# An order written out by hand: 1,087 operations of a convolution and gMLP block put in another sequence

## The chip, the cores and the metric

The kernel runs on one core of one Trainium2 chip. The time is the device time of that core in microseconds (us), from the start of the launch to its end; the figure quoted is the median of three executions. A profile was taken of one further execution, and all rows and lines of a trace come from that one.

The engines of the core are called by the letters that the kernel itself uses: P is TensorE (matrix products and transposes), D is VectorE, A is ScalarE, G is GpSimd (POOL in the profile), and S is SyncE, which here only issues transfers. Each engine takes its instructions strictly in the order in which it was given them, and waits at an instruction whose operands are not ready, with everything behind it.

## What is computed

The sequence has S = 2048 tokens and D = 640 channels, the batch is one, the gMLP's inner half is Fh = 864, and everything outside is bf16. Cut to what matters:

```python
mod = (silu(c) @ w_mod).reshape(6, D)            # sa, ca, ga, sb, cb, gb
h = layernorm(x) * (1 + ca) + sa                 # x is A_q
k4 = sum(shift(k, t) * shift_k[:, 3 - t] for t in range(4))
kv = k4 * v
y = irfft(rfft(kv, 2 * S) * rfft(ssm_k, 2 * S))[:S] + kv * ssm_D
x = x + ga * h * y
h = layernorm(x) * (1 + cb) + sb
z = gelu(h @ w_in)                               # 2048 x 1728
g = w_sp @ layernorm(z[:, 864:]) + b_sp[:, None]  # the token mix
out = x + gb * ((z[:, :864] * g) @ w_out)
```

## The kernel before

**How the work is cut.** The long convolution is a Fourier transform written as matrix products. The 640 channels are five units of 128 channels (units 0 to 4). A unit's k passes four taps (a product with four diagonal matrices), is multiplied by v, regrouped by a transposing transfer, and then goes through a first transform stage, eight steps of the second stage with the product by the filter's transform, the inverse stage, and a last stage that is multiplied straight into the gate h·ga. The filter ssm_k takes the same two first stages, with ssm_D added to its first element, which stands for the term kv·ssm_D. The tables of sines and cosines are worked out on the chip at the start.

The gMLP works on four groups of four token tiles of 128. A group's layer norm, its transpose hT, the modulation by 1 + cb and sb, the product with w_in (in blocks of 128 tokens by 432 features), GELU, the statistics of the second half and its normalization follow one another. The token mix w_sp·z is done as products over 2x2 blocks, seven for every pair of output tiles in place of eight; for it sums and differences of the blocks of w_sp and of z are made first. The first pair's seven products belong to the list described next; the other seven pairs and most of the product with w_out follow it in an ordinary loop.

**What sets the order.** The program first only records 1,087 operations: each with a number (its place in the recording), the engines that may run it, what it reads and writes, and the tiles that it allocates. The list ORDER at the top of the file then gives the sequence: the letter says which engine runs the operation, the number which operation it is. `Plan.run` walks through the list, asserts that all that an operation depends on was put out before it, and issues it:

```python
for e, i in order:
    o = self.ops[i]
    assert e in o["eng"] and done.issuperset(o["deps"]), (e, i)
    o["fn"](engines[e])
```

So the list holds no times and no priorities. It decides for each engine in which order its operations come, for operations that may run on several engines which of them does it, and, since a tile of a tag with n buffers is handed out again after n allocations, which earlier readers a new tile waits for. The number of buffers of every tag is in `SLOTS`; the ones named below are `pu` and `pz` (two PSUM tiles each), `sm` (two), `s1` (one), `T` (two) and `KH` (seven).

**The operations that are named later**, by number:

- Start. P1034 and other numbers from 1033 to 1038 are filling matmuls. S2, S3, A1 and G5/D6 fetch D, c and the shift taps (A1 is a transfer that ScalarE issues) and widen D; P7, P8 and P9 turn them, A10, A11 (D_col) and A12 copy them out; A4 is one Silu activation on a scratch value (line 786). D13 to D22 make the tables of the first stage, D27 is the padding of unit 0's k and A28 its diagonal matrices of taps. Loads of k and v S23 to S26, S39, S40, S52, S64, S65 and S77; taps and v (P29 to D36 for unit 0); regrouping transfers kx (S37, S38, S51, S63, S76, S88). S89, S90, S93, S95, S97 and S99 load ssm_k, D91, D92, D94, D96, D98 and D100 add D_col to it.
- Tables of the second stage, numbers 101 to 127, in four chunks: turns (D104, D110, D116, D122), subtraction (the number after), two sines each on ScalarE, a sign (G108, G114, G120, G126) and a negation (G109, G115, G121, G127; line 357). P134, P137, P140 and P143 with A135 and their like copy and negate them into the inverse's tables. A133 is one GELU activation on a scratch value (line 815); it loads ScalarE's function table for GELU ahead of its first use.
- Convolution. P146 to A157: first stage of the filter of unit 0, with copies out of PSUM; P158 to A173: its second stage, with copies into `KH` tiles; P174 to D184: first stage of kv of unit 0. From P186 on come the steps: forward product (P186), product with the filter on VectorE (D187, line 470), where wanted two sums (csum, G188 and G189; lines 479 and 480), the inverse product (P190) and the copy zc (A191; line 504). Units 1 to 4 hold the numbers 228 to 523 in the same way; D515 is the last filter product.
- S524 to S527 load x in quarters (640 KB each, S527 the last), D528 to 549 are the first layer norm's statistics (ln1), 550 to 565 its normalization (xn). S566, S571, S576, S581, S584 and S587 load w_mod in sixths, and 567 to 591 make the six modulations of it; ghm, 592 to 599 and later, puts h, 1 + ca, sa and ga together for each unit; res adds the finished unit to x, ln2 takes the statistics of the sum.
- Transition. P716 to D723 flip the last unit's result and copy it out, P724 to P750 are its last stage, D728 to D731 and D737 multiply it into the gate, D732 to D742 add it and take statistics.
- z. For group 0: 759 to 777 statistics and normalization, P765, P766, P778 and P779 transposes, D767 to A771 and D780 to A784 the modulation of the two halves, then a product on TensorE followed by its GELU on ScalarE, in pairs (P785 and A786, P788 and A789, P792 and A793, P813 and A814, P815 and A816, P817 and A818, ...; lines 944 and 946). Groups 1, 2 and 3 turn hT by a transfer (S845, S911, S977) and modulate it with 846 to 850, 912 to 916 and 978 to 982, on three engines. G829, G895, G961 and G1027 are the rstd of the second half (line 955, two instructions on GpSimd: lines 189 and 190), D1028 the number that goes with G1027, and 1029 to 1032 group 3's normalization zn (line 967).
- Mix. S1039 to S1044 load transposed tiles of w_sp, S1045 the bias, S1046 w_out; D1055 to D1062 and D1063 to D1070 are sums of blocks of w_sp and of z (line 1021; D1063 and D1064 T1, D1065 and D1066 T2, D1067 and D1068 T3, D1069 and D1070 T4); P1071, P1073, P1075, P1077, P1078, P1082 and P1084 the first pair's seven products (line 1036), each with eight matmuls.

Of the kernel before, what the change touches and what calls it, by code (L numbers as in the profile page):

```python
# [37 lines left out]


ORDER = """  # L40
D0 P1034 A1 P7 D18 D128 D13 D15 A4 S89 D14 A16 D101 S2 G5 D6 P8 G102 D103 D116 D117 A10 A11 P1038 A28 A129 S90 D91 D17
P1035 A118 A119 S23 P146 P149 D104 S25 D105 A106 A107 D27 P1036 A147 P29 A148 P31 G108 S24 A150 G109 S26 D92 P155 D110
D111 A112 D151 A113 A156 G120 G121 P152 A154 A153 G114 D30 D32 G115 D20 P33 D122 D123 A124 A157 A125 G126 S524 D34 P35
D36 S525 D528 D529 D530 P1033 P158 A159 P162 A163 P134 P164 A135 A165 P166 A167 P137 D19 A21 P140 D141 P168 G127 S93
A169 P170 S37 S38 A171 D138 P172 A173 D94 P228 A229 D22 P174 A176 G139 P177 A179 D531 D175 D178 P234 S39 D235 G136 G41
P180 A181 D182 D532 P183 P230 A184 G53 A185 P186 D187 G142 A231 P202 D203 G42 P43 A533 D130 P232 G188 D189 S40 D44 P45
D46 S52 P196 D197 A534 G198 G199 S527 P160 A161 P190 A191 A233 P49 D50 P47 G54 D48 P212 P204 P248 S3 A535 P200 A205 P9
A249 P143 D213 G214 G215 D543 A12 G67 G131 G132 P222 A144 G145 D223 P55 D56 P192 D193 D536 G537 P59 D60 A544 A545 S51
P57 P252 A253 D58 P206 D207 G208 G209 P194 A201 S566 P218 D219 D538 G550 G551 P254 A195 A255 S526 D539 D540 P567 A568
S95 P569 A570 P258 A259 P216 P236 A237 P242 A243 G224 G225 P256 D257 P238 A217 A239 A541 P61 D62 S571 D96 S65 P210 S64  # L50
G66 P240 A241 P260 P220 D261 A211 G554 A546 P302 A303 P292 G555 G556 G557 A221 P574 G262 G263 D542 G552 D293 D547 P246
A247 P226 A227 S63 P572 P286 D287 D288 D553 P304 A305 D573 P264 A265 P250 A251 G78 P294 A295 P308 A309 D575 D652 G548
D549 G562 D592 P296 D297 G289 P276 A558 G298 P68 P306 S576 D277 P72 D615 P244 P290 A133 D559 A307 P270 D271 P326 A245
D69 P278 A291 G563 G564 P316 D73 A327 A565 D598 A317 P266 P328 A329 A279 D267 G299 P300 D301 P577 P314 S97 A315 P330
A331 G272 G273 D594 P324 A325 G613 D650 D578 S77 D593 D614 P70 D71 A560 A561 G617 P310 A311 P332 A333 G595 D714 D671
P280 D281 P74 D98 P579 D596 D75 P322 A323 P274 P350 A79 D351 G282 P376 A377 G283 P344 D345 D580 G654 A275 P268 A269
P334 D335 P378 G599 A379 P80 D597 P312 S600 A313 D81 P284 G346 G347 P320 P601 D602 A285 A321 P380 G336 G337 D708 G709
P366 A381 P370 D367 D371 P82 P382 A383 P318 G619 A319 P603 P338 P348 A349 A339 D83 S76 P388 A389 P400 D604 P605 D606
A401 S99 D100 P360 D361 P352 A353 P386 A387 P402 D620 G618 G372 G373 A403 P607 D608 P374 D375 P398 A399 G362 P354 G363
D355 G610 D356 G357 D616 P404 G653 A405 P364 P86 P384 A365 G656 P406 A407 D87 A385 P340 D341 P84 P368 D85 P408 P414  # L60
D409 A369 P450 P342 A451 P390 S621 P622 D415 G710 A391 G711 G677 D623 G410 G411 P454 A455 P418 P396 D419 A343 P624
P358 S581 P452 A397 D625 A453 G651 G420 D421 P392 P440 A393 P626 D627 P412 D441 G657 P456 A359 P428 G678 A413 G655
A457 D429 G430 G431 P628 D629 G630 P416 A417 P394 A395 P422 D423 S88 P474 A475 P464 A465 D635 P444 D445 G446 P582 A583
P480 A481 D636 P424 D425 P442 A443 D675 G676 D637 P458 A459 G447 P476 A477 D638 P434 D435 P426 D427 P472 A473 S658
P659 D660 P478 A479 P432 P466 P661 A433 P482 P448 A467 D609 D632 A449 D662 P663 G436 G437 P438 A439 P462 A463 D483
P498 D664 P665 D499 G673 G484 G485 P518 P486 D519 P502 D503 D504 P500 A501 G674 P460 A461 P468 A469 D666 P488 D489
A487 S584 G672 P585 A586 P508 G520 G521 P522 G505 A523 G668 D509 P492 D493 P506 A507 P470 A471 S679 P680 D681 P514
D515 G510 P490 A491 G511 G494 G495 P512 G715 G667 D634 A513 P682 D683 P516 A517 D631 P684 D685 P496 S757 D639 D633
P686 D687 D688 D690 A497 P720 A721 P716 G693 P722 P718 D717 P724 D719 P726 A723 P727 D689 P725 D728 G698 D729 D730
D759 D731 D760 G761 D696 D732 D733 D692 D762 G763 D735 A764 S587 P588 A589 P736 P1037 P590 A591 D734 D691 D772 D773  # L70
G774 P750 P765 D737 D738 D767 D769 D768 P766 A771 A770 D775 P743 D741 D837 G712 D697 P792 D751 S758 A777 P815 A816
D694 G776 P779 A783 A784 D742 P785 D739 D835 A786 D695 D740 P778 D836 D838 D752 A793 D713 D744 D745 G703 G839 D840
G841 G842 D843 P788 D782 A789 D781 D780 G612 D794 P795 A796 P817 P819 D670 D797 D669 D702 D700 D706 D611 G640 D642
A844 S845 D749 A818 P799 A800 G847 D641 D644 A820 D747 D902 P821 G846 D705 D701 D801 D645 D699 A822 P823 A824 D643
D904 P802 A803 D804 P806 A807 P825 A826 D805 A848 P813 A850 P827 A828 P809 A810 D849 A814 P851 A852 D746 P875 A876
D901 P879 A880 P858 A859 D748 D903 D790 D787 D811 P872 A873 D808 G905 D906 P865 S1046 P889 A866 A890 D648 P881 D704
A882 D756 D646 D812 D753 D967 D907 D909 G908 D754 D1050 P861 A862 D1047 P854 A855 D867 P893 A894 S1042 P883 A884 D798
G910 S911 P887 A888 A916 P891 A892 D877 P868 A869 D647 D968 P885 A886 D755 D969 D649 D707 D970 D1051 G971 D972 S1040
D791 S1039 A973 D976 D914 D975 D974 D853 D1052 G912 S1045 G913 G915 D856 P959 A960 P917 A918 D857 G829 D830 S977 G982
D874 D878 P947 A948 D834 D831 D860 D832 D833 D1063 D870 P920 A921 P924 A925 P938 A939 S1044 D863 D864 P931 S1041 D1055  # L80
D1056 P941 A942 D1058 D926 D979 G980 P927 A928 A932 G978 D1048 P953 D919 D933 D871 D929 P934 D940 P949 A954 D922 A981
P1000 D1054 P997 D923 S1043 A935 D936 G895 D896 D899 D1059 A950 P983 D930 A998 D999 D1060 A1001 D1002 A984 D943 D944
A898 A900 P993 A994 P1007 A1008 D937 D1057 G961 D897 D1064 D962 P1004 D985 D963 P990 P986 A987 D988 D989 A991 D992
D995 D996 A1005 D1006 P951 D1003 A952 A964 D965 P1025 P1015 A1016 D1009 D1010 A1026 D966 D1067 G1027 D1028 P955 A956
P945 A946 P957 D1030 P1021 A1029 P1013 D1032 A1022 A1014 P1071 P1073 A958 D1031 D1068 P1082 D1065 D1066 P1078 D1069
D1070 A1072 P1075 D1079 A1074 D1083 P1077 D1076 D1080 P1084 P1011 A1012 D1085 P1017 A1018 P1019 A1020 S1081 D1062
S1086 D1049 P1023 A1024 D1053 D1061
"""


# [1143 lines left out]
```

## The time and the profile before

| what | value |
|---|---|
| median of three executions | 312.26 us (312.03 to 312.69) |
| the profiled execution | 312.08 us |
| span of its instructions | 310.0 us |
| P186, the first forward product of unit 0, starts | 23.68 us |
| D515, the last filter product, starts | 119.08 us |
| D767, the first modulation of z, starts | 131.52 us |
| P1071, the first tile product, starts | 188.71 us |
| the last operation of the list on TensorE ends | 205.05 us |

The span runs from the first instruction to the last; the device time has 2.08 us more, around it. The busy time of an engine is a sum over the whole span, while the limits change by stage: what counts for a change in one stage is which engine is full there and which wait ends last there. The profile page cuts the span into 40 slices with the busy tenths of each engine. The view by windows gives the busy time of each engine in stretches that one chooses. Overlapping matmuls are pipelined, so that TensorE's work is best taken from the spacing of starts: 0.44 us for a forward block, 0.89 for a block of taps, 0.91 for a block of z, 1.46 for one tile product. In a timeline row the columns are start, duration, engine, line, operation, output and inputs with their shapes, and in brackets the idle time before it and what ended that.

### The profile page before, as it was taken

Reading aid. Unit: us, or ns where it says so; the run is one execution under the profiler, and the core shown is the slowest. Engines: PE = TensorE matmul, PEld = TensorE weight load, DVE = VectorE, ACT = ScalarE, POOL = GpSimd, SP = SyncE. Lnnn points to the kernel's source line nnn. Section 1 sums busy time; section 2 is a strip of 40 time slices with the busy share of each in tenths; the row PEclk is TensorE's granted clock in tenths of the full one; section 3 lists DMA queues with packets and bytes.
Section 4 is the critical chain, followed back from the end, with each engine's and each line's share of the span. In section 5 each row is a group of like instructions: output and inputs, shape, how many; then the busy total and the mean of one; then the engine's idle time right before and its main releaser. Section 6 shows DMA issues by size and latency. Waiting matters only on the chain.

```text
span 310.0 us, 6894 instructions
## 1 busy us (share of the span) xinstructions
PE 296.2 (96%) x2746; PEld 207.1 (67%) x2746; DVE 259.6 (84%) x528; ACT 157.0 (51%) x282; POOL 123.0 (40%) x157
## 2 busy tenths in 40 slices
PE   6989999999999998999999997999999999999996
PEld 2779898889999887755554553555565656555564
DVE  7999899999899999999969998957676858567474
ACT  5899899897969755476665684040101010010100
POOL 2663788859899696676342522000000000000000
PEclk9999999999999999999999999999999999999999
DMA  7999989986396779204999900092939395640614
GB/s 147 275 176 250 244 220 252 225 169 132 26 231 134 173 134 323 76 3 85 216 175 147 183 2 2 0 140 63 194 89 187 63 176 111 129 102 0 104 30 114
DMA packets 122963, 42.63 MB, mean 137 GB/s; under 512 B 108751, under 2 KB 122932, under 8 KB 122932
## 3 DMA queue, kind: packets, MB, share of 16 engines
q1 hardware_dynamic: 122778, 42.16, 64.6%
q8 instruction: 21, 0.34, 0.4%
q14 instruction: 10, 0.08, 0.1%
q10 hardware_dynamic: 154, 0.05, 0.1%
HBM read 16.11 MB, written 2.62 MB: 60 GB/s over the span
## 4 chain that ended last, share of the span: by engine, by line
PE 63%; DVE 25%; DMA 4%; issue 3%; ACT 2%; POOL 2%; POOLq 1%; DVEq 0%; ACTq 0%
PE ps L1036 23%; PE pu L244 12%; PE po L1160 10%; PE pz L244 8%; PE sm L244 4%; DVE st L949 3%; DVE Tf L463 3%; DMA ZT<-Z 3%; PE s L244 2%; PE pz L1036 2%; DMA KH<-in_c_dram 2%; DVE T L463 2%; DVE X L570 2%; DVE gh L684 1%; DVE st L603 1%
## 5 line engine op out<-in xcount | busy, mean ns | idle before, releaser
L244 PEld LDWEIGHTS <-Z 128*128 128x128 bf16 x320 | 30.9, 98 | 28.2 <-POOL Z L920 1.5
L244 PE MATMUL pu<-X,M 128*128 128x128 bf16 (+1 forms) x480 | 45.7, 237 | 1.9 <-ACT X L247 0.7
L244 PEld LDWEIGHTS <-M 128*128 128x128 bf16 x480 | 37.3, 98 | 6.3 <-issue 3.1
L1036 PEld LDWEIGHTS <-S 128*128 128x128 bf16 x256 | 25.0, 98 | 24.0 <-issue 2.4
L1042 ACT COPY m<-ps 128x432 f32<-128x432 f32 x7 | 3.6, 519 | 72.7 <-PE ps L1036 72.7
L477 POOL TENSOR_TENSOR W<-Tf 128x256 bf16<-128x256 f32 x45 | 33.2, 759 | 10.2 <-DVE Tf L463 8.3
L247 ACT CAST X<-s 128x1024 bf16<-128x1024 f32 x30 | 30.6, 1021 | 4.9 <-PE s L244 4.5
L1160 PE MATMUL po<-w_o,uT 128*128 128x320 bf16 (+2 forms) x231 | 32.7, 295 | 0.0
L244 PE MATMUL pz<-big,Z 128*128 128x432 bf16 x160 | 32.4, 346 | 0.3 <-POOL Z L920 0.3
L244 PE MATMUL pu<-big,Z 128*128 128x432 bf16 x160 | 32.3, 346 | 0.3 <-DVE Z L894 0.3
L463 DVE TENSOR_TENSOR Tf<-pu,KH 128x1024 f32<-128x1024 f32 x25 | 30.2, 1216 | 2.0 <-PE pu L244 1.7
L1036 PEld LDWEIGHTS <-wT 128*128 128x128 bf16 x192 | 18.7, 98 | 15.2
L1160 PEld LDWEIGHTS <-uT 128*128 128x128 bf16 (+1 forms) x231 | 22.2, 98 | 9.7
L244 PEld LDWEIGHTS <-G 128*128 128x128 bf16 x330 | 24.8, 98 | 1.7 <-issue 0.2
L247 ACT CAST Z<-pz 128x512 bf16<-128x512 f32 x36 | 20.9, 596 | 7.7 <-PE pz L244 7.5
L247 ACT CAST KH<-pu 128x512 bf16<-128x512 f32 x40 | 23.4, 595 | 2.1 <-PE pu L244 1.8
L1036 PE MATMUL ps<-X,wT 128*128 128x432 bf16 x112 | 22.7, 346 | 0.0
L1036 PE MATMUL ps<-T,S 128*128 128x432 bf16 x112 | 22.7, 346 | 0.0
L1036 PE MATMUL ps<-X,S 128*128 128x432 bf16 x112 | 21.6, 346 | 0.0
L244 PEld LDWEIGHTS <-X 128*128 128x128 bf16 x288 | 17.9, 97 | 4.8 <-issue 1.6
L244 PE MATMUL sm<-dg,big 128*128 128x128 bf16 x320 | 20.5, 219 | 0.2 <-DVE gca_bf L671 0.2
L244 PEld LDWEIGHTS <-big 128*128 128x128 bf16 x320 | 18.8, 98 | 0.6 <-issue 0.3
(189 smaller groups left out, 563.5 us busy)
## 6 DMA issues: line engine op xcount, KB each, us to landing
wm<-in_w_mod_dram SPq DMA_DIRECT2D x6, 800.0 KB, 5.6
xt<-in_A_q_dram SPq DMA_DIRECT2D x4, 640.0 KB, 7.3
out_dram<-ot SPq DMA_DIRECT2D x15, 160.0 KB, 2.0
big<-in_B_w_in_dram SPq DMA_DIRECT2D x2, 1080.0 KB, 5.9
X<-in_A_ssm_k_dram SPq DMA_DIRECT2D x4, 512.0 KB, 7.0
big<-in_A_v_dram SPq DMA_DIRECT2D x2, 1024.0 KB, 6.3
w_o<-in_B_w_out_dram SPq DMA_DIRECT2D x6, 160.0 KB, 3.0
X<-in_A_ssm_k_dram SPq DMA_DIRECT2D x2, 256.0 KB, 3.8
```

What stands on the lines that cost most here:

```text
L244: nc.tensor.matmul(o, lhsT=w, rhs=x, start=start, stop=stop)
L247: (e.copy if e is nc.scalar else e.tensor_copy)(dst, src)
L463: e.tensor_tensor(T_[:], (tl[pu] if src is None else tl[src])[:, :, :, None, :].to_broadcast(shape), tl[KH][:, :, None, :, :].to_broadcast ...
L477: e.tensor_tensor(tl[W][:, :, o, :], T_[:, :, 0, o, :], T_[:, :, 1, 1 - o, :], op=ALU.add if o else ALU.subtract)
L570: e.tensor_tensor(tl[kv][:].rearrange("p c (n g) -> p n c g", g=8)[:, 4 * i:4 * i + 4], tl[ps][:].rearrange("p a (c g) -> p a c g", g=8), ...
L603: e.bn_stats(out=st[:, a, :], in_=xt[:, n, a * HS:(a + 1) * HS])
L684: lambda e, vec=vec, o=o: e.tensor_tensor(gvu, gvu, vec[:, None, d0:d0 + du].to_broadcast([P, TB, du]), op=o),
L949: op("D", "stz", lambda e, i=i, n=n, fc=fc: e.bn_stats(out=stz[:, n, fc, :], in_=tl[z2][:, i, fc * FC:(fc + 1) * FC]), r=[(z2, (i, fc))], ...
L1036: nc.tensor.matmul(ps[:, :FC], lhsT=lhs[:, s_, :], rhs=rhs(s_), start=(s_ == 0 and not more), stop=(s_ == HT - 1), skip_group_check=more)
L1042: nc.scalar.copy(part[p, m][:], part[p, BANK[m]][:, :FC])
L1160: nc.tensor.matmul(ps[:, :hi - lo], lhsT=uTs[t][:fsz[ft], ft, :], rhs=w_o[:fsz[ft], ft, lo:hi], start=(ft == 0), stop=(ft == NFT - 1))
```

## The change

Only the string ORDER is changed. All 1,087 operations stay, with the same instructions; the number of buffers, the loop behind the list and everything else are the same. TensorE keeps its 305 operations and SyncE its 53; 97 others change their engine, so that VectorE has 357 in place of 354, ScalarE 248 in place of 240 and GpSimd 124 in place of 135. Almost every line is new. What is moved:

- At the start A4 stands ahead of A1 on ScalarE, A28 and A118 ahead of A11; the chunks of the second stage's tables and the first stage's products come in another order, and the negation A115 was G115.
- On SyncE S26 goes ahead of S25 and S24; S93 ahead of S524 and S525; S3 ahead of S527; S64 and S63 ahead of S65; S88 ahead of S581. At the end the order is S845, S1046, S1045, S1039, S911, S1041, S1040, S977, S1042, S1043, S1044, and before it was S845, S1046, S1042, S911, S1040, S1039, S1045, S977, S1044, S1041, S1043.
- In the convolution unit 1 to 4's pieces are interleaved otherwise with each other and with ghm, res, xn, ln1 and ln2. Changed in their engine: csum from VectorE to GpSimd four, back five; zc to ScalarE four, to VectorE two; ghm to GpSimd eight, to VectorE twelve; res to GpSimd four, to VectorE four; xn one to VectorE from GpSimd, one from ScalarE, one from VectorE to GpSimd and one there from ScalarE, three from GpSimd to ScalarE; ln1 two to ScalarE and one to VectorE.
- A133, between two units' work before (in the line with A307), now stands behind group 0's first blocks of z, after A786, A789 and others.
- In z the blocks, GELUs, statistics and normalizations of the groups are put in another order; of zn seven go from VectorE to ScalarE and two the other way; hmod2 changes its engine in eight places, zx in five, the first stage's copies in thirteen. Group 3's statistics (its last D989 to D1010) stand ahead of D1063 and D1067, the sums of T1 and T3, and these stand directly ahead of G1027; D1065, D1066 and D1064 come after P1071. A1022, A958, A1014 and A1016 stand ahead of A1030.

The diff, cut to the lines with the operations that are spoken of:

```diff
--- before
+++ after
@@ -38,53 +38,53 @@
 ORDER = """
-D0 P1034 A1 P7 D18 D128 D13 D15 A4 S89 D14 A16 D101 S2 G5 D6 P8 G102 D103 D116 D117 A10 A11 P1038 A28 A129 S90 D91 D17
-P1035 A118 A119 S23 P146 P149 D104 S25 D105 A106 A107 D27 P1036 A147 P29 A148 P31 G108 S24 A150 G109 S26 D92 P155 D110
-D111 A112 D151 A113 A156 G120 G121 P152 A154 A153 G114 D30 D32 G115 D20 P33 D122 D123 A124 A157 A125 G126 S524 D34 P35
-D36 S525 D528 D529 D530 P1033 P158 A159 P162 A163 P134 P164 A135 A165 P166 A167 P137 D19 A21 P140 D141 P168 G127 S93
-A169 P170 S37 S38 A171 D138 P172 A173 D94 P228 A229 D22 P174 A176 G139 P177 A179 D531 D175 D178 P234 S39 D235 G136 G41
-P180 A181 D182 D532 P183 P230 A184 G53 A185 P186 D187 G142 A231 P202 D203 G42 P43 A533 D130 P232 G188 D189 S40 D44 P45
-D46 S52 P196 D197 A534 G198 G199 S527 P160 A161 P190 A191 A233 P49 D50 P47 G54 D48 P212 P204 P248 S3 A535 P200 A205 P9
-A249 P143 D213 G214 G215 D543 A12 G67 G131 G132 P222 A144 G145 D223 P55 D56 P192 D193 D536 G537 P59 D60 A544 A545 S51
...
-S95 P569 A570 P258 A259 P216 P236 A237 P242 A243 G224 G225 P256 D257 P238 A217 A239 A541 P61 D62 S571 D96 S65 P210 S64
...
-D549 G562 D592 P296 D297 G289 P276 A558 G298 P68 P306 S576 D277 P72 D615 P244 P290 A133 D559 A307 P270 D271 P326 A245
...
-A457 D429 G430 G431 P628 D629 G630 P416 A417 P394 A395 P422 D423 S88 P474 A475 P464 A465 D635 P444 D445 G446 P582 A583
...
-D515 G510 P490 A491 G511 G494 G495 P512 G715 G667 D634 A513 P682 D683 P516 A517 D631 P684 D685 P496 S757 D639 D633
...
-D694 G776 P779 A783 A784 D742 P785 D739 D835 A786 D695 D740 P778 D836 D838 D752 A793 D713 D744 D745 G703 G839 D840
...
-D904 P802 A803 D804 P806 A807 P825 A826 D805 A848 P813 A850 P827 A828 P809 A810 D849 A814 P851 A852 D746 P875 A876
-D901 P879 A880 P858 A859 D748 D903 D790 D787 D811 P872 A873 D808 G905 D906 P865 S1046 P889 A866 A890 D648 P881 D704
...
-G910 S911 P887 A888 A916 P891 A892 D877 P868 A869 D647 D968 P885 A886 D755 D969 D649 D707 D970 D1051 G971 D972 S1040
-D791 S1039 A973 D976 D914 D975 D974 D853 D1052 G912 S1045 G913 G915 D856 P959 A960 P917 A918 D857 G829 D830 S977 G982
-D874 D878 P947 A948 D834 D831 D860 D832 D833 D1063 D870 P920 A921 P924 A925 P938 A939 S1044 D863 D864 P931 S1041 D1055
...
-P1000 D1054 P997 D923 S1043 A935 D936 G895 D896 D899 D1059 A950 P983 D930 A998 D999 D1060 A1001 D1002 A984 D943 D944
-A898 A900 P993 A994 P1007 A1008 D937 D1057 G961 D897 D1064 D962 P1004 D985 D963 P990 P986 A987 D988 D989 A991 D992
-D995 D996 A1005 D1006 P951 D1003 A952 A964 D965 P1025 P1015 A1016 D1009 D1010 A1026 D966 D1067 G1027 D1028 P955 A956
-P945 A946 P957 D1030 P1021 A1029 P1013 D1032 A1022 A1014 P1071 P1073 A958 D1031 D1068 P1082 D1065 D1066 P1078 D1069
...
+A4 A1 S89 D0 G102 P1036 P1035 P7 D13 D15 S2 S90 D14 A16 D101 A10 D103 D116 D117 P1033 S23 G5 D6 A28 A118 D17 D104 D105
+P8 A11 D92 A119 D91 A106 D110 D111 A107 P1034 D18 D20 S26 P146 A113 S25 D122 D123 A147 A148 P149 A151 A150 G27 P29 D30
+A112 G114 D19 A124 P31 D32 P155 A156 P152 D153 S24 P33 D34 P35 D36 S93 A157 G108 G109 A154 D94 P158 A21 D22 S524 P134
+A125 P228 D229 A115 G120 D128 A159 A135 D528 P164 A165 P162 A163 G121 P168 A169 P166 A167 S525 D532 P234 A235 G126
+D529 G127 P172 A173 P170 A171 P137 S37 P174 P177 S38 D176 A175 D179 D138 G139 P1038 P140 D141 P183 A178 D184 S39 A530
+G41 P180 D181 G42 G136 D531 P230 G54 G142 A182 A185 P186 D187 G188 S40 A231 P202 S52 D203 P232 A533 P43 G189 P45 G53
+D44 S3 D46 A233 A534 A535 S527 P196 D197 G198 G199 P248 A249 P47 D48 P49 P190 P9 A12 P160 A161 P212 D50 S51 D536 G537
+A191 P200 D213 G214 A543 G215 A201 P222 P55 D223 G224 G225 S566 D56 P218 P204 P192 D219 D193 P59 D538 G554 G555 D60
+A544 A129 P252 A253 P206 D207 G131 G132 P143 D144 A205 D556 P236 A237 P254 A255 S526 P57 P194 P258 P242 G145 S95 A545
...
+D592 G288 G289 P290 A291 P328 A329 G594 P310 A311 S65 D69 A562 P280 D73 D281 G299 P300 P74 D75 P270 A301 P330 A331
...
+D608 G609 P408 D409 D85 P390 A391 P86 D87 P454 A455 P414 S621 P622 D623 P364 P396 A397 A365 G673 D415 P452 P624 S88
...
+G674 G714 D493 P470 P680 D681 P514 A471 D515 P506 A507 P682 G510 G511 P512 P516 D683 D632 P684 D649 D685 G494 G495
...
+A777 D695 D740 D836 P743 P785 A786 D742 D838 P788 A789 P817 A818 D835 G776 P779 D741 D837 A783 D715 D751 D752 P813
...
+D781 P806 D745 D749 P799 A800 A807 D669 D698 D700 G640 G611 D642 P802 A803 D755 D643 P809 D703 A133 S1046 G849 S1045
...
+D748 D699 D790 D746 D901 D903 P858 D902 G905 S1039 D794 P872 D906 D648 A824 D801 D1047 P868 A907 A873 G910 P881 A869
+D909 D908 S911 G916 D646 D797 A882 D798 D1054 D1053 D967 A859 P885 A886 D705 P875 P854 D754 S1041 P883 D970 A876 D787
...
+P887 A888 P879 D811 A880 D808 D812 D804 D805 G913 P893 D863 D864 A894 D856 D972 D973 D975 G829 P917 A918 D976 D974
...
+A897 P949 A950 D982 G978 P983 A984 P1000 A1001 P1007 D933 D834 D1052 P1004 A1008 A1005 D1058 D936 P993 A898 A994 P997
+A998 D919 D923 D944 D937 G961 D1002 D985 D1009 P986 D1006 D962 D964 D965 D1051 A963 P990 A991 S1042 D999 D1003 D1059
+A987 A966 P957 S1043 D1010 P1021 D988 A1022 D989 A958 P1013 A1014 D995 P1015 D992 D996 A899 D1063 D1067 P959 A960
+G1027 D1028 D1031 A1016 P945 D1029 A1030 S1044 P1025 A1026 A1032 P1071 A1072 P951 A952 D1064 P1073 D1065 A946 D1066
...
 """
```

## The prediction

> **What bounds the kernel now.** Operations are named as in the list ORDER, by engine letter and number. I first read the page's totals, then the busy time by stage, cut at the first convolution product (D187, 24.58 us; its TensorE block P186 starts at 23.68), the last product (D515, 119.08), the first modulation of z (D767, 131.52), the first tile product (P1071, 188.71) and the list's end (205.05).
>
> ```profile
> PE 296.2 (96%) x2746; PEld 207.1 (67%) x2746; DVE 259.6 (84%) x528; ACT 157.0 (51%) x282; POOL 123.0 (40%) x157
> ```
>
> ```profile
> 0.00:23.68 23.68, 19.54 (x196) 14.23 (x197) 21.81 (x70) 18.60 (x40) 11.81 (x27) 1.00 0.97 200
> 23.68:119.08 95.40, 92.56 (x1300) 85.33 (x1301) 90.18 (x136) 80.56 (x138) 75.84 (x89) 1.00 0.84 183
> 119.08:131.52 12.44, 11.23 (x226) 9.54 (x224) 11.69 (x31) 5.82 (x10) 8.15 (x11) 1.00 0.54 202
> 131.52:188.71 57.19, 56.57 (x335) 30.12 (x332) 53.14 (x151) 38.51 (x71) 25.34 (x31) 1.00 0.58 110
> 188.71:205.05 16.34, 14.20 (x78) 7.53 (x77) 14.96 (x24) 4.99 (x9) 1.89 (x1) 1.00 0.24 24
> 205.05:310.00 104.95, 102.12 (x623) 60.32 (x621) 67.83 (x120) 8.51 (x15) 0.00 (x0) 1.00 0.52 107
> ```
>
> Columns: stretch, length, busy PE, PEld, DVE, ACT and POOL, granted clock, DMA share, GB/s. TensorE is full in the convolution (92.6 of 95.4) and in z (56.6 of 57.2), VectorE follows closely (90.2, 53.1), and the clock never drops. The list's TensorE work can't shrink, since the same instructions stay on the same engine. From the start-to-start times in the timeline (0.44 us a forward block, 0.89 taps, 0.91 a z block, 1.46 a tile product) it is 189.1 us; it begins at 1.64 and ends at 205.05, so 14.3 us are waits. A new order can only change those. Next a line of the chain of waits (the load of c, on the path with 5.43 us), and the timeline at the function table's load and at the wait before the mix.
>
> ```profile
> 27.57 5.43 DMA KH<-in_c_dram
> ```
>
> ```profile
> 56.28 1.28 ACT L815 ACT_TABLE_LOAD   x1
> ```
>
> ```profile
> 188.31 0.33 POOL L189 TENSOR_SCALAR rstdz<-mvz 128x4 f32<-128x4 f32 x1 [5.09 <-DVE mvz L953]
> 188.69 1.06 DVE L1021 TENSOR_TENSOR X<-X,X 128x1728 bf16<-128x1728 bf16 x1
> 188.72 1.89 POOL L190 TENSOR_TENSOR rstdz<-rstdz,mhalf 128x4 f32<-128x4 f32 x1
> 190.91 1.11 ACT L964 ACTIVATE X<-X,nmrz,rstdz 128x864 bf16<-128x864 bf16 x1 [4.20 <-DVE nmrz L958]
> 191.92 0.93 ACT L943 ACTIVATE G<-pz 128x432 bf16<-128x432 f32 x2
> 192.48 1.62 PE L1036 MATMUL pz<-T,S 128*128 128x432 bf16 x8 [2.15 <-ACT G L943]
> ```
>
> The last fence is the largest single wait: P1073 needs the PSUM tile that GELU A1022 empties; A1022 stands behind A1029, which waits for the last group's rstd (G1027), ready at 190.61. Against its place in the TensorE sum P1073 is 2.3 us late.
>
> **The start: +1.3.** A4 and its table load now stand ahead of A1, which fetches the shift taps from ScalarE's queue. Issued at 0.71 before, A1 goes out after 1.28 + 0.20 us of load and activation, near 2.1 (0.71 if the queue runs ahead of the load, so this term's lower end is +0.6). With the 2.6 us that the like-sized load of D took to land, P7 starts at 4.75, not 4.32. Then A28 (1.28) and A118 (0.5) precede A11, so D_col comes at 6.95 instead of 5.44; D92 and D91 wait 0.5 us for it, D110 and D111 (1.3) follow, A113 waits for D111 until 8.8, and the copies A147, A148, A151, A150 (0.5 each) queue behind it. Walked on with rows of this trace: P158 starts at 13.9 (14.53 before), but A115 (the negation moved from POOL, 1.0), A135 (1.0) and five KH copies fill ScalarE until 20.9, and P174 waits for A173's tile. D176 then waits 0.6, D181 ends at 24.85, and P186 starts at 24.95 instead of 23.68: +1.3 (upper end 1.4). D187 starts at 25.85 instead of 24.58.
>
> **The load of c: -0.9.** It now goes ahead of the 640 KB S527, though behind D187, which frees its slot: about 27.05, against 27.57. Landing took 5.43 with S527 ahead; at some 250 GB/s that is 2.6 us less, so it lands near 30. P9 comes at 31.2 and waits no more; before it was 0.9 late. Lower end -0.9, upper 0.
>
> **The convolution: +0.6.** Most of the reshuffle is here. Between D187 and D515 VectorE loses 10.0 us of work (zc and csum to ScalarE and POOL, seven ghm, an ln1) and gains 12.8 (eleven ghm, two res, five csum, two xn, three ln2 pulled forward): +2.8 at start-to-start times. POOL loses 5.7, and ScalarE's GELU table load leaves. In the second row above VectorE idles 5.2 us and TensorE 2.8. If every idle microsecond of VectorE took up work, the stretch would lose at most some 1.0, since TensorE's sum stays; if none did, it would gain 2.8. VectorE ran nearly without gaps from 24 to 72 us, and idled mostly from 72 to 105, where TensorE had no waits; so about 2.2 of 2.8 fits there, and +0.6 is left. The SP queue's moves (kx of unit 2 ahead of v, kx of unit 4 ahead of w_mod, XK1 ahead of x) bring forward what TensorE reads and delay x by some 2 us, which D528 meets only at 17.5; I cost them at nothing. Without that cover each is one transfer's landing, 5 to 7 us, less what TensorE has queued. So D515 comes at 119.08 + 1.3 - 0.9 + 0.6, +1.0 in all. From D515 to D728 VectorE has 6.64 us in both orders, and from D728 to D767 0.4 less: nothing.
>
> **The GELU table: +1.1.** A133, which loads it at 56 us under other work, now follows the first GELUs, so the load falls to A786. A777 ahead of it waits for D775, which now has D738, D739, D697 and D696 (some 1.1 us) ahead of it, so ScalarE is free 1.4 us after P785 ends. A786 would be done 0.5 later, 1.9; with the row's 1.28 it is 3.2. TensorE has P788, P817 and P779 to do meanwhile (0.9 + 0.9 + 0.4 = 2.2), then P813 needs A786's tile: about 1.1 late with the signal. Behind A786 stand A789, A818 and A783 (0.5 each), which P792, P815 and P806 want later than P813 wants its own. In the row the activation follows the load at once, at 57.57. The Trainium skill's page "ScalarE: Activation LUTs", section "What ACT_TABLE_LOAD costs", adds a drain of about 1.38 us to a load of the same length. By the page the term would be +2.5 and the forecast 312.7 instead of 311.3. The trace shows no such gap, so I take 1.1; the range's ends are 0 (the load hidden) and 2.5.
>
> **The turns of hT: -0.8.** Before, waits at P815 (0.46), P917's group (0.61), P1000 (0.08) and P986 (0.23) add to 1.4. P785 keeps 0.46. With TensorE later by the table load, G913, now behind G971, ends about 0.1 after P917's turn, and the other two go. S911 stands behind S1046, S1045 and S1039 (3.2 + 0.6 + 2.9 us of issue), which just fits; if not, G916, G914, G971 and G913 wait with it. Ends -1.0 and +0.8.
>
> **The mix: -2.3.** D989, D1010, D996 and D1003 now end near P1025's middle, some 3 us earlier against TensorE than before, and A1022, A958, A1014 and A1016 stand ahead of A1030. P1071, P1073, P1078 and P1082 each find their tile and sums. But T1's and T3's sums (D1063, D1067, 1.06 each) now run beside G1027. In the fence, its second step took 1.89 instead of the 1.08 median while one such sum ran. The page "SBUF — State Buffer", section "SBUF: two separate sides", says that VectorE and GpSimd share a port pair as an exclusive lock, held for a whole instruction. By one row G1027 takes 2.3 us; by the rule, with both sums ahead of it, up to 3.0, and D1028 moves 0.7 later. A1030, D1066 and P1078 still have that much, so I keep -2.3; its ends are -2.3 and 0. Past the list the loop is the same and its operands are ready.
>
> **Sum.** 1.3 - 0.9 + 0.6 + 1.1 - 0.8 - 2.3 = -1.0. The profiled execution took 312.08, a span of 310.0 and 2.08 around it; it becomes 311.08. The median of the runs shown, 312.26, is 0.18 above it: 311.3.
>
> **Rivals.** VectorE becomes the bound (slower): the load of c then wins nothing, the start counts whole, and the 2.8 us stay: +4.1 at D515, less 2.0 behind it, is 314.4 (312.8 to 314.6). It decides once D515 comes after 120.9. For it: the 90.2 of 95.4; against it: POOL's lighter load and the late idle time. The wait before the mix comes back through the port or ScalarE's order of zn and GELUs: up to 2.3 more, 312.2 to 313.6. Against it: two further GELUs of margin. Nothing is lost early: the start is made up for by D515, and the turns and the mix give their 3.1, with the table load hidden behind another wait or not: 309.2 to 310.3. The unchanged spacing of TensorE's blocks speaks for it, the first walk against.
>
> **How the numbers follow.** The main case has 0.40 and its own range 310.4 to 312.1; VectorE's rival 0.30, the mix's 0.13, the early one 0.17. A measurement tells 0.2%, 0.62 us, from no change, so faster ends at 311.64 and slower begins at 312.88. Faster: 0.27 of the main case and 0.17; same: 0.13 of it and 0.04 of the mix's; slower: 0.30 and 0.09. The range from 309.5 to 314.6 takes in the rivals' ends but for the fastest tip.
>
> **What would show it.** Right: P186 near 24.9; no wait for c at P9; D515 near 120; an ACT_TABLE_LOAD just ahead of the first GELU with P813 late by a microsecond; TensorE without a gap between the first two tile products. Wrong: D515 past 121 with VectorE gapless, or a new wait at P1073 or P1078.

## The result, and the profile after

The changed kernel takes 307.71 us, the kernel before, run beside it, 312.14; the ratio is 0.9856 (95% interval 0.9839 to 0.9873). It is 4.4 us faster, where 1.0 was forecast, and lies below the range, which began at 309.5. The totals of the page after, and its busy time by stage, cut at the same five instructions as before (P186, D515, D767, P1071, the list's end):

```profile
PE 294.8 (96%) x2746; PEld 207.1 (68%) x2746; DVE 253.9 (83%) x529; ACT 162.7 (53%) x290; POOL 111.0 (36%) x146
```

```profile
0.00:23.61 23.61, 19.84 (x197) 14.34 (x198) 20.90 (x67) 20.52 (x44) 8.30 (x24) 1.00 0.99 207
23.61:117.51 93.90, 92.13 (x1307) 85.55 (x1308) 89.99 (x147) 77.94 (x135) 72.18 (x85) 1.00 0.85 188
117.51:128.96 11.45, 10.43 (x207) 8.73 (x205) 11.04 (x30) 6.03 (x9) 7.25 (x9) 1.00 0.50 186
128.96:185.59 56.63, 55.30 (x339) 30.13 (x337) 49.90 (x148) 44.08 (x79) 23.28 (x30) 1.00 0.57 111
185.59:200.54 14.95, 14.95 (x83) 8.02 (x82) 13.81 (x21) 5.58 (x10) 0.00 (x0) 1.00 0.16 31
200.54:305.50 104.96, 102.12 (x623) 60.32 (x621) 68.24 (x121) 8.51 (x15) 0.00 (x0) 1.00 0.53 106
```

The last row is that of before to 0.01 us: all 4.5 us were won in the list, which ends at 200.54 instead of 205.05. The first row is as long as before (23.61, 23.68), all the others but the last are shorter, and TensorE has no wait at all in the mix. TensorE's waits, taken as in the prediction from the spacing of its blocks, fall from 14.2 to 9.7 us. By the steps of the prediction:

| step | predicted | measured in the trace |
|---|---|---|
| start, up to P186 | +1.3 | -0.1 |
| load of c, P9 | -0.9 | -0.9 |
| convolution, P186 to P720 without P9 | +0.6 | -0.7 |
| transition, P720 to P765 | 0 | -0.5 |
| GELU table, P813 | +1.1 | +1.5 |
| turns of hT, P815 to P986 | -0.8 | -1.4 |
| mix, P1073 | -2.3 | -2.3 |
| sum (measured: the list's end) | -1.0 | -4.5 |

The start, on ScalarE and its queue, with the row of TensorE's P186:

```profile
0.72 1.28 ACT L786 ACT_TABLE_LOAD   x1 [0.72 <-PEq L1218]
0.89 0.56 ACTq L777 DMA_DIRECT2D KH<-in_A_shift_k_dram  x1
2.01 0.20 ACT L786 ACTIVATE warm<-warm 128x1 f32<-128x1 f32 x1
...
23.61 1.04 PE L244 MATMUL pu<-X,M 128*128 128x256 bf16 x12 [1.46 <-DVE X L247]
```

A1's transfer goes out at 0.89, in the middle of the table's load, though it stands behind A4: for the issue of a transfer the strict order on an engine, as told at the start, does not hold here. P186 waits 1.5 us for D181. Then the GELU table, and P813 behind it:

```profile
132.28 1.28 ACT L943 ACT_TABLE_LOAD   x1
133.58 0.53 ACT L943 ACTIVATE X<-pu 128x432 bf16<-128x432 f32 x1
...
134.16 1.07 PE L244 MATMUL pu<-big,Z 128*128 128x432 bf16 x5 [1.33 <-ACT X L943]
```

And the place of the old wait before the mix, where both tile products now stand without an idle time ahead of them, and GpSimd's rstd (lines 189 and 190) is done 1 us before the first of them starts:

```profile
182.39 1.00 DVE L1021 TENSOR_TENSOR T<-X 128x1728 bf16<-128x1728 bf16 x1
182.56 0.88 POOL L189 TENSOR_SCALAR rstdz<-mvz 128x4 f32<-128x4 f32 x1 [6.52 <-DVE mvz L953]
183.53 1.01 POOL L190 TENSOR_TENSOR rstdz<-rstdz,mhalf 128x4 f32<-128x4 f32 x1
183.85 1.06 DVE L1021 TENSOR_TENSOR X<-X,X 128x1728 bf16<-128x1728 bf16 x1 [0.46 <-ACT X L964]
...
185.59 1.62 PE L1036 MATMUL pu<-X,wT 128*128 128x432 bf16 x8
187.05 1.08 PE L244 MATMUL pz<-big,Z 128*128 128x432 bf16 x5
187.97 1.26 PE L1036 MATMUL pz<-T,S 128*128 128x432 bf16 x6
```

### The profile page after: what moved, and what is told of

Same layout as the page of the kernel before. It is cut to its first block, busy times and chain, and to the rows that moved or that the text cites. A ratio compares the mean times of both kernels' runs of the same rounds, so it can differ in the third digit from the quotient of the medians.

```text
span 305.5 us, 6890 instructions
## 1 busy us (share of the span) xinstructions
PE 294.8 (96%) x2746; PEld 207.1 (68%) x2746; DVE 253.9 (83%) x529; ACT 162.7 (53%) x290; POOL 111.0 (36%) x146
## 4 chain that ended last, share of the span: by engine, by line
PE 80%; DVE 8%; DMA 5%; SPq 3%; ACT 2%; issue 1%; DVEq 0%
PE ps L1036 23%; PE pu L244 18%; PE pz L244 15%; PE po L1160 10%; PE sm L244 7%; PE s L244 3%; DMA ZT<-Z 3%; DMA xt<-in_A_q_dram 3%; PE pz L1036 2%; PE pu L1036 1%; SPq L532 1%; DVE Tf L463 1%; DVE X L247 1%; DVE st L727 1%; DVE gh L701 1%
## 5 line engine op out<-in xcount | busy, mean ns | idle before, releaser
L477 POOL TENSOR_TENSOR W<-Tf 128x256 bf16<-128x256 f32 x44 | 31.8, 745 | 10.7 <-DVE Tf L463 6.4
L244 PEld LDWEIGHTS <-G 128*128 128x128 bf16 x330 | 24.7, 98 | 2.0 <-DVE T L463 0.4
L247 ACT CAST Z<-pz 128x512 bf16<-128x512 f32 x38 | 22.3, 593 | 6.0 <-PE pz L244 5.8
L949 DVE BATCH_NORM_STATS2 st<-X 128x6 f32<-128x432 bf16 x32 | 18.0, 587 | 4.2 <-ACT X L943 4.2
```

Source lines behind the costliest of these rows:

```text
L244: nc.tensor.matmul(o, lhsT=w, rhs=x, start=start, stop=stop)
L247: (e.copy if e is nc.scalar else e.tensor_copy)(dst, src)
L477: e.tensor_tensor(tl[W][:, :, o, :], T_[:, :, 0, o, :], T_[:, :, 1, 1 - o, :], op=ALU.add if o else ALU.subtract)
L949: op("D", "stz", lambda e, i=i, n=n, fc=fc: e.bn_stats(out=stz[:, n, fc, :], in_=tl[z2][:, i, fc * FC:(fc + 1) * FC]), r=[(z2, (i, fc))], ...
```

## The experiments

Every kernel was timed together with the kernel before on one chip; the latter's executions reached from 310.8 to 314.4 us, so that a ratio is known to 0.2 or 0.3%, and the traces decide what is smaller. Diffs show the pieces of ORDER that are moved.

**Is the transfer held up by the table's load?** The kernel before with A4 ahead of A1:

```diff
-D0 P1034 A1 P7 D18 D128 D13 D15 A4 S89
+D0 P1034 A4 A1 P7 D18 D128 D13 D15 S89
```

> The kernel before with A4, and so the first table load, ahead of A1, the transfer that ScalarE issues. The prediction's step: the transfer waits for load and activation, goes out near 2.1 in place of 0.71, P7 starts at 4.75 or later and the rest of the start is pushed by up to 1.4. The theory from the trace after, where A1's transfer went out at 0.89 in the middle of the load (0.72 to 2.00): it goes out at 0.9, P7 starts between 3.7 and 4.4, P158 no later than 14.6, the time is that of before.

Measured: 312.10 against 312.44, ratio 0.9971 (0.9952 to 0.999). A1's transfer went out beside the load:

```profile
0.72 1.28 ACT L786 ACT_TABLE_LOAD   x1 [0.72 <-PEq L1218]
0.89 0.56 ACTq L777 DMA_DIRECT2D KH<-in_A_shift_k_dram  x1
```

With that the prediction's premise for the start falls. P7 started at 4.32, to the hundredth as before; this alone would show little, since P7 stands behind six filling matmuls (P1034) until then in both. P158 came at 15.54, later than I expected, because three blocks from 7.4 us on (P146, P149 and P1036) took twice their spacing in this execution (0.42 more each); three other traces with the unchanged start show the same. P186 came 1.0 later by it (24.68), and at P409 0.2 was left (89.69 for 89.50): P9, later too, found its load landed. So in the old order the start and the load of c are not two separate terms.

**Is the place at 56 us free for the GELU table?** The kernel before with A133 in ScalarE's idle time ahead of A764:

```diff
-P244 P290 A133 D559
+P244 P290 D559
...
-P726 A723 P727
+P726 A723 A133 P727
```

> The kernel before with one operation moved: A133 stands behind A723, in ScalarE's idle time of 4 us ahead of A764. The theory that the load at 56 us held up A307 and with it TensorE: the waits at P244, P270 and P326 (0.26 + 0.25 + 0.31 us) go, D515 comes 0.8 earlier and the time is 311.3. The prediction's own assumption, that the load lies under other work at 56 us: no wait goes, and the time stays at 312.1.

Measured: 312.49, ratio 1.0019 (0.999 to 1.0049). P244 and P270 still wait 0.25 each, P326's 0.31 is gone and P324 waits 0.22 instead. The load at 56 us was nearly free, as the prediction had it; my later theory falls. This trace shows something else, in the stretch behind the wait at P1073; the windows' columns are those of the stages above, then TensorE's rows:

```profile
190.70:193.00 2.30, 0.21 (x2) 0.00 (x0) 1.68 (x5) 1.52 (x3) 0.48 (x1) 1.00 0.01 4
193.00:197.50 4.50, 4.45 (x16) 2.00 (x16) 4.50 (x5) 1.87 (x5) 0.00 (x0) 0.65 0.00 0
```

```profile
193.05 1.79 PE L1036 MATMUL pz<-T,S 128*128 128x432 bf16 x8 [2.14 <-ACT G L943]
194.63 3.09 PE L1036 MATMUL pz<-X,S 128*128 128x432 bf16 x8
```

After 2.1 us of idle time the granted clock is 0.65 over the next 4.5 us, and a tile product takes 3.09 instead of 1.62: 1.5 us more behind the wait.

**The same in the changed kernel**, where P813 waits for the load: A133 behind A719.

```diff
-P722 D717 A719 D723
+P722 D717 A719 A133 D723
...
-P809 D703 A133 S1046
+P809 D703 S1046
```

> The changed kernel with one operation moved: A133 stands behind A719, in ScalarE's idle time of 2 us ahead of A589, so that the GELU table is loaded before the first GELU wants it. Theory: the wait of 1.49 us at P813 goes, the time is 307.7 - 1.5 = 206.2 + 100.0, that is 306.2. Rival: the wait is only handed on, since A777 behind D775 is late too, and the next ones (P792, P815) wait in its place: 307.2 to 307.7.

Measured: 306.32, ratio 0.9836 (0.9802 to 0.987). P813's wait is gone and none of its size takes its place: from P785 to P813 it is 3.0 us instead of 4.45. P879 and P927 wait 0.4 together, which they don't in two later runs with the same move.

**Is the start worth more?** The wait at P186 attacked:

```diff
-A175 D179 D138 G139 P1038 P140 D141 P183
+A175 D179 G42 P1038 P140 P183
...
-S39 A530 G41 P180 D181 G42 G136 D531 P230 G54 G142 A182 A185
+S39 G41 P180 D181 D138 D141 G139 G136 P230 G54 G142 A185 A182
...
-S40 A231 P202
+S40 A231 A530 P202
...
-D44 S3 D46 A233
+D44 S3 D46 D531 A233
```

> The changed kernel with the wait of 1.6 us at P186 attacked: D138 and D141 (copies for the inverse's tables, 0.68 each) stand behind D181 in place of ahead of D184, A530 (a statistic of x, 1.65) behind A231, D531 behind D46, A185 ahead of A182, and G42 ahead of G139. Theory: P186 comes about 1.0 us earlier (22.6 in place of 23.6), the stretch behind it is bound by TensorE, so that the gain lasts to the end: 307.7 - 1.0 = 306.7. Rival, the prediction's picture of a VectorE that is nearly full up to D515: the gain is taken up by D515 and the time stays at 307.7.

Measured: 308.47, ratio 0.9894 (0.9867 to 0.9922), no gain. P186 comes at 22.93 instead of 23.61, but P248 then waits 1.41 for A233, behind the moved A530, and P659 waits 1.87 for its transfer. VectorE runs almost without a gap from 16 to 45 us; work that is moved behind P186 is met again.

**The old order up to z, the new from there:**

```diff
-G774 P750 P765 D737 D738 D767 D769
+D737 G712 S758 D694 G612 D670 D645 D649 P765 D767 D768
```

> The old order up to the first transpose of z (P765), the new order from there, A133 at its new place behind the first GELUs. If the gain behind z is what the prediction's three terms say (GELU table +1.1, turns -0.8, mix -2.3), this kernel takes 312.1 - 2.0 = 310.1. If the table's load at 56 us had a price of its own, some 0.8 us in TensorE's waits at P244, P270 and P326 that the prediction set at nothing, it takes 312.1 - 2.0 - 0.8 = 309.3. In both cases the wait at P813 (1.5 us) is there and the wait at P1073 (2.3 us) is not.

Measured: 312.56, ratio 1.0019 (0.9998 to 1.004). It tells nothing of the terms: the seam puts D737, D694, D670, D645 and D649 directly ahead of D767, which comes 2.6 us late, P785 waits 2.16, and TensorE then runs 5.5 us at a clock of 0.50, so that P813 has no wait either. The wait at P1073 is gone, and P244 and P270 wait as before.

**The changed kernel again, with three variants beside it.** The yardstick:

> The changed kernel itself, unaltered, beside the next three on the same chip, as their yardstick. Expected 0.9856 of the time before, within 0.2%.

Measured: 307.41, ratio 0.9851 (0.9824 to 0.9878). P659 waited 1.64 in this trace and 0.64 in the first; the gate tile's transfer landed after 9.5 and 8.5 us.

The engines of before in the new order (53 letters, for example):

```diff
-A558 D265 P72 D267 A315 A327 P324 A325 G652 D592 G288
+A558 A265 P72 D267 A315 A327 P324 A325 D652 D592 D288
```

> The changed kernel's order with the engines of before for the 53 operations between P186 and P720 that had changed theirs (csum, ghm, xn, zc, res, ln1 and a few more). The prediction's step, that the new engines give VectorE 2.8 us more work there and cost 0.6: without them the kernel is 0.6 faster than the changed one, 307.1, and VectorE idles more before D515. The rival from the trace after: VectorE's instructions that both kernels have took 2.8 us less in the changed kernel, because fewer of them ran into one of GpSimd's, and the moves between engines are part of that; without them those instructions get longer again, TensorE's waits between 54 and 77 us come back, and the kernel is 0.3 to 1.3 slower than the changed one, 308.0 to 309.0.

Measured: 324.24, ratio 1.0393 (1.0361 to 1.0425), far beyond both. TensorE's waits up to P720 are 23.4 us, against 7.8 in the changed kernel. It doesn't tell which engine is to blame, only that order and engines belong together.

The load of c late:

```diff
-D44 S3 D46 A233 A534 A535 S527 P196
+D44 D46 A233 A534 A535 S527 S3 P196
```

> The changed kernel with S3, the load of c, behind S527 as before. The prediction's step: P9 is 0.9 late again and all behind it, up to 308.6, if TensorE's stretch carries it to the end. Rival: the gain of the load of c was not kept up to D515, since P659 waits for a transfer (its gate tile ZT) 70 us later and takes up what came before: 307.7, with P9 late and P659's wait of 0.64 us shorter by as much.

Measured: 307.76, ratio 0.9865 (0.9835 to 0.9895). In the trace P9 waits again:

```profile
31.52 0.17 PE L244 MATMUL sm<-ident,KH 5*128 5x5 bf16 x1 [1.33 <-DMA KH<-in_c_dram]
```

It is 1.5 us late. Against the first trace of the changed kernel 0.9 of that is left at the list's end, and P340 and P659 wait 0.4 less; against the second, in which P186 came 0.4 later and P659 waited 1.64, nothing is left. So the wait at P9 hangs on this one move, as the prediction had it; that it costs the time 0.9 is not shown, and the time measured is the rival's.

The table in the gap and a milder change of the start (A530 stays, D531 behind D203):

```diff
-A175 D179 D138 G139 P1038 P140 D141 P183
+A175 D179 G42 P1038 P140 P183
...
-D181 G42 G136 D531 P230 G54 G142 A182 A185
+D181 D138 D141 G139 G136 P230 G54 G142 A185 A182
...
-S52 D203 P232
+S52 D203 D531 P232
```

> The changed kernel with A133 behind A719 as in the run with the table in the gap, and in addition D138, D141 and G139 behind D181, D531 behind D203, G42 ahead of G139 and A185 ahead of A182; A530 stays where it was. Theory: P813's wait of 1.49 us goes and P186 comes 0.5 us earlier, which TensorE keeps: 2.0 us less than the changed kernel, 305.7. Rival: P659 takes up the half microsecond of the start by waiting longer for its transfer: 1.5 less, 306.2.

Measured: 306.28, ratio 0.9811 (0.978 to 0.9841): the rival's time, but not by the rival's cause. P186 comes 0.85 earlier, P47 then waits 0.85 for D44 behind D531, and at D261 0.06 is left; P659 waits 0.60 (0.64 in the first trace of the changed kernel).

**What shortened VectorE?** Between D187 and D515 its instructions that both kernels have there took 85.2 us before and 82.2 after. D98, 16 elements per partition, shows why, with GpSimd beside it; before:

```profile
68.11 1.16 DVE L401 TENSOR_TENSOR X<-X,D_col 128x16 bf16<-128x16 bf16 x1
...
68.03 1.15 POOL L684 TENSOR_TENSOR gh<-gh,gsa_bf 128x512 bf16<-128x512 bf16 x1
```

It ends at 69.27, GpSimd's instruction at 69.18. Two parts of D547, 128x1 each, before:

```profile
49.95 0.64 DVE L614 TENSOR_TENSOR sums<-mv 128x1 f32<-128x1 f32 x1
50.63 0.82 DVE L615 TENSOR_TENSOR mv<-mv,sums 128x1 f32<-128x1 f32 x1
...
49.17 1.41 POOL L477 TENSOR_TENSOR W<-Tf 128x256 bf16<-128x256 f32 x2
50.57 0.87 POOL L631 TENSOR_SCALAR gh<-xt,rstd,nmr 128x640 bf16<-128x640 bf16 x1
```

They end at 50.59 and 51.45, GpSimd's at 50.58 and 51.44. In the whole stretch eleven of VectorE's instructions took more than 0.12 us longer before than their shortest length in any trace of this study, 4.7 us in sum; ten of them, with 4.4 us, ended within 0.3 us behind a GpSimd instruction that ran beside them. The first test moves D98 and D547 to where GpSimd is idle:

```diff
-D293 D547 P246 A247 P226 A227 S63 P572 P286 D287 D288
+D293 P246 A247 P226 A227 S63 P572 P286 D287 D547 D288
...
-P70 D71 A560
+P70 D71 D98 A560
...
-P74 D98 P579
+P74 P579
```

> The kernel before with two of VectorE's operations moved by one place or a few, to where GpSimd works on nothing: D547 (the last step of ln1's second half, six small instructions, 2.34 us in the trace before against 1.03 in the changed one) behind D287, and D98 (adding D_col to unit 3's filter, 1.16 against 0.22) behind D71. Theory: those lengths were waits for a running GpSimd instruction; VectorE gets 1.3 us free at 50 and 0.9 at 68, and the waits of TensorE that hang on it shrink or go: P68 (0.34), P244 (0.26), P270 (0.25), P376 (0.39), P334 (0.24), 1.0 to 1.5 in all, so that D409 comes at least 1.0 earlier than it else would after P9, and the time is up to 1.2 less than before, if P659's transfer does not take it up. The prediction's picture, in which VectorE's work has the length that the rows of before show: D547 and D98 stay as long, none of the waits moves, the time is that of before.

Measured: 311.35, ratio 0.9997 (0.9975 to 1.0019). D547 takes 1.02 and D98 0.23, but TensorE gains nothing: now D596 meets GpSimd (1.35 instead of 0.41), D297 stands behind D549, which waits for G548, and P244 and P334 wait 0.57 and 0.64. The second puts the products first:

```diff
-D652 G548 D549 G562 D592 P296 D297 G289 P276 A558 G298 P68 P306 S576 D277
+D652 G548 P296 D297 G289 D549 G562 P276 A558 G298 P68 P306 S576 D277 D592
...
-D596 D75 P322 A323 P274 P350 A79 D351
+P322 A323 P274 P350 A79 D351 D596 D75
```

(with D98 and A133 moved as above.)

> The kernel before with VectorE's products put ahead of small operations that wait for GpSimd: D297 ahead of D549 (which waits for the rstd G548), D592 behind D277, G289 ahead of G562; D351 ahead of D596 and D75; D98 behind D71; and A133 behind A723. Theory, after the run that moved D547 and D98 and only handed the waits on to the next small operation: TensorE's waits at P244 (0.26), P270 (0.25), P376 (0.39) and P334 (0.24) were due to what stood ahead of the products on VectorE, and all four go: D409 comes 1.1 earlier than before, and the time is 1.1 less, 0.3 to 0.5 more of it lost or won at P326, P68 and P659. Rival: VectorE has too much to do in this stretch in any order, the waits come back a few blocks later, D409 is where it was and the time that of before.

Measured: 312.36, ratio 1.0 (0.9977 to 1.0022). The rival: P266, P350, P80, P312 and P320 wait 2.5 us together, D592, D671 and D596 are long now, and from P9 to P409 this trace takes 1.7 us more than before. Two runs that leave work out settle what this left open. In the class that walks the list:

```diff
-            o["fn"](engines[e])
+            if i not in LEFT_OUT:
+                o["fn"](engines[e])
```

> The kernel before with twelve of VectorE's ghm left out (594, 592, 593, 596, 597, 598, 614, 615, 650, 652, 671 and 714, all between 54 and 74 us, 5.5 us of VectorE in sum), so that part of the gate misses its factors; order, engines and all other work are as before. Theory: TensorE's waits between 54 and 78 us are VectorE's, which is full there; without the twelve the waits at P244, P270, P376, P334 and P318 go (0.26 + 0.25 + 0.39 + 0.24 + 0.14 = 1.3), D409 comes 1.3 earlier and the time is 1.0 to 1.3 less than before. Rival: they hang on ScalarE and on the order in which blocks reuse their PSUM tiles; then less than 0.4 of them goes.

Measured: 310.59, ratio 0.9957 (0.9927 to 0.9987). The waits at P244, P270, P376 and P334 are gone, P318's is 0.29 instead of 0.14. D409 comes 1.9 earlier, of which 0.84 is P9, whose load landed in time here.

> The kernel before with the 21 ghm left out that GpSimd runs ahead of D515 (24.7 us of GpSimd), so that part of the gate misses its factors; VectorE's list is as before, instruction by instruction. Theory: VectorE's small instructions are long where they meet a running GpSimd instruction; with fewer of these D98 falls from 1.16 to 0.22, D597 from 0.85 to 0.42 and D616 from 0.95 to 0.41, while D547 keeps its 2.34 (it met csum and xn, which stay); P376 and P334 lose their waits, P244 and P270 keep theirs, and D409 comes 0.6 to 0.9 earlier. Rival: the lengths are VectorE's own, and nothing on VectorE or TensorE moves before 75 us.

Measured: 310.56, ratio 0.9951 (0.9923 to 0.9979). VectorE's list is that of before, and the row of D98 is (its lines stand four further down):

```profile
68.56 0.22 DVE L405 TENSOR_TENSOR X<-X,D_col 128x16 bf16<-128x16 bf16 x1
```

D597 falls to 0.42, D547 keeps 2.32; P376, P334 and P318 lose their waits (0.8 in all), P244 and P270 keep theirs, and from P9 to P409 it is 0.8 us less; P49 and P9 had lost 0.5 before that, so that D409 itself comes only 0.3 earlier, a miss. D616 stays at 0.95, another miss: it meets a csum, which stays. So VectorE's fullness sets TensorE's waits here, and GpSimd's instructions are part of VectorE's length.

**The best of it.** A133 in the gap, and S581, an 800 KB load, off the gate tile's transfer:

```diff
-S621 P622
+S581 S621 P622
...
-P392 A393 S581 P626
+P392 A393 P626
```

(with A133 moved as above.)

> The changed kernel with A133 behind A719 (the GELU table loaded in ScalarE's idle time) and S581, a load of 800 KB of w_mod, ahead of S621 in place of just ahead of S658. Theory: S658's transfer of the gate tile took 8.5 us to land because that load ran beside it; alone it lands 2 us sooner, P659's wait (0.64 in the profiled run, 1.64 in the repeated one) goes as well as P813's 1.49: 2.1 to 3.1 less than the changed kernel, 304.3 to 305.6. Rival: the transfer is as slow by itself, and only P813's wait goes: 306.2.

Measured: 305.62, ratio 0.9797 (0.9777 to 0.9817): faster than both kernels, against the changed one by 1.8 us. P813's wait is gone. P659 still waits 0.52 and its transfer took 8.4 us, so the load was not why it takes that long in the first trace. The traces side by side say when it does matter: in the four in which S581 went out 1.9 to 2.3 us ahead of S658, the transfer landed after 9.5 to 9.9 us; in the other twelve, with 3.4 us or more between them, after 8.3 to 8.5. That is a comparison, not a test of its own.

## Why the prediction was wrong

Of the some 3.5 us between forecast and trace the start gave 1.4, the convolution 1.3, the turns 0.6 and the transition 0.5; the GELU table took 0.4 back.

Three steps hold. **The mix**: the wait of 2.3 us at P1073 is gone, and G1027 took 1.98 beside the sums of T1 and T3, nearer to the row's 2.3 than to the 3.0 by the rule. **The load of c**: issued at 26.64, no wait at P9. **The GELU table**: its load sits just ahead of the first GELU, the activation follows at once (133.56, 133.58; the drain of 1.38 us that the page cited in the prediction states is not there), and P813 is late by 1.5 where 1.1 was said; the three runs with A133 in the gap take that back.

**The start (+1.3) rests on a false premise**, "A1 goes out after 1.28 + 0.20 us of load and activation". The transfer went out at 0.89 while the table was loading, and its last semaphore update in the trace is at 3.03, 2.1 us later, where the landing of D's load had given 2.6. P7 did not wait for it, neither before (last update at 2.14) nor after: it follows the filling matmuls without an idle time. Their rows, with P7's behind them, before:

```profile
1.64 2.74 PE L244 MATMUL s<-ident 128*128 128x512 bf16 x6 [1.64 <-DVE ident L288]
4.32 0.29 PE L244 MATMUL sm<-ident,KH 5*128 5x5 bf16 x4
```

After, with two fewer of them, which the prediction did not count:

```profile
1.65 2.10 PE L244 MATMUL s<-ident 128*128 128x512 bf16 x4 [1.65 <-DVE ident L288]
3.69 0.29 PE L244 MATMUL sm<-ident,KH 5*128 5x5 bf16 x4
```

P7 starts at 3.69, not 4.75, and the 1.1 us go through the walk nearly unchanged: P158 12.69 for 13.9, D181's end 23.46 for 24.85, P186 23.61 for 24.95. From its second step on the walk was right to 0.3 us. One pair of traces is a thin measure here: P186 came at 23.7 or at 24.7 with the old start (four traces each), and at 23.2 to 24.1 in six with the new one. The reserve for this case, an end of +0.6, changed only that row and did not walk on.

**The convolution (+0.6) was wrong in its sign.** "VectorE loses 10.0 us of work and gains 12.8" took lengths from rows of before, with the waits for GpSimd that are in them. Against the shortest length that each instruction has in any trace of this study, VectorE's between D187 and D515 were 5.6 us too long before, and 2.0 after; in the second quarter of that stretch 3.3 and 0.7. The added work was there, and more of it than said (by the shortest lengths 11.4 us lost and 16.0 gained), but so was room: VectorE is busy 90.0 of 93.9 us, as long as before. TensorE's waits from 54 to 78 us (1.9) vanish. The Trainium skill's page "SBUF — State Buffer", section "SBUF: two separate sides", says that the two engines share a port pair as an exclusive lock, held for a whole instruction, and that a VectorE instruction with two inputs in SBUF needs it against a GpSimd instruction that reads SBUF. The rows of D98 and D547 above are of that kind and agree, to 0.01 us in D547. The mix does not agree in full: D1067, with both inputs in SBUF, ran its usual 1.06 us from 183.85 on, in the middle of G1027's second step, which took 1.01, not longer than its median of 1.08 before. I applied the rule at the mix, where it decided nothing, and not where small VectorE instructions meet GpSimd's. The two runs that leave work out show both links; that they are the whole of the 1.3 us between forecast and trace is not shown, since order and engines can't be undone one by one (324 us).

**The transition (0)** won 0.5, 0.33 of it at P724, whose copy D717 comes sooner, and **the turns** gave 1.4 for 0.8: the 0.46 that P785 was to keep went too. Neither was tested alone.

Of the rivals, "nothing is lost early" had the direction and most of the places, but not the gain in the convolution, and its 309.2 to 310.3 was missed too. VectorE did not become the bound: D515 came at 117.5.

## What to carry to other kernels

Before work is moved to VectorE, sort its rows by the shortest length that the same instruction has: what lay above that here was mostly a wait for GpSimd (4.4 of 5.6 us), which changes with the order, and moving a single operation only handed it to the next small one. A table load belongs where ScalarE waits anyway: behind a copy with a gap after it, it cost nothing, ahead of the first use 1.5 us. In a walk by hand, a premise on which all later steps hang needs its other answer walked to the end as well.

## What was not expected

A wait of some 2 us on TensorE can cost more than its length. In five traces the granted clock was 0.50 to 0.65 for 4.5 to 5.5 us after waits of 2.1 to 2.3 us (at P1073, P659 and P785), worth 1.7 to 2.7 us more; in three others, that of the kernel before among them, the wait of 2.3 us at P1073 had no such sequel. The mean clock of those five executions is 0.989 to 0.995, that of the three 1.0. Of the 96 executions of the kernel before beside the experiments 24 have a mean of 0.995 and a median time of 313.4 us, the other 72 have 1.0 and 312.0; that it is the same sequel in all 24 is not shown. The changed kernel has no wait above 1.7 us in its two traces, and no such stretch from the convolution on.
